# Eighty-seven short idle matmuls for five long ones, and two zeroings moved ahead of a maximum, in a fused convolution and maxout layer

## The chip, the cores and the metric

The kernel runs on one core of a Trainium2 chip. The time is device time in microseconds (us) of one execution; for the kernel before it is the median of three runs. The profile is of one further execution, with a span of 454.9 us from the first instruction to the last. TensorE multiplies matrices, VectorE (DVE), ScalarE (ACT) and GpSimd (POOL) work element by element, and SyncE (SP) issues most of the transfers, which run on the core's 16 DMA engines.

## The reference, cut to what matters

The input `x` has 8 sequences of 4160 tokens with 192 channels. First comes a causal convolution along the sequence: 8 heads of 24 channels, 7 taps a head, the taps being the softmax of `weight`. Then comes a maxout layer over all 33,280 tokens:

```
w = softmax(weight)                                  # 8 heads x 7 taps
y[s, h, :] = sum over k of w[h, k] * x[s - 6 + k, h, :]   # zero ahead of a sequence
h = maximum(maximum(y @ w1, y @ w2), y @ w3)         # 192 -> 768
out = h @ w_out                                      # 768 -> 192
```

The output is float32.

## The kernel before, in words

**Blocks.** The tokens are cut into 65 blocks of 512. Each block goes through four steps: load and cast its input to 16 bits, convolve, first layer with maxima (`h`), second layer (`po`, `o`) and store.

**The algebra.** The kernel doesn't form three products. With `wd` holding `w1 - w3` and `w2 - w3`, it computes `h = max(relu(y (w1 - w3)), y (w2 - w3))`, and adds `y (w3 w_out)` in the second layer, where the small matrix `w3 w_out` (`m16`) is made once by `transpose_w3` and `make_m`. ScalarE does the relu out of PSUM (line 494, tile `r`), VectorE the maximum (line 495, tile `h`), which also releases the PSUM buffer of the second product (`lq`).

**Convolution.** It is a matmul with a banded matrix (`band`), made at the start from the softmax by 38 small matmuls (line 280) and copies by ScalarE and VectorE (line 284). Blocks 0 to 3 are "dense": their input is cast to 16 bits into `xz` (line 211), 80 matmuls of line 382 (tile `D`) convolve them channel-major, and the result `yd` is used directly; `cross` makes the copy of two channel groups on the other half of the partitions that the first layer needs. From block 4 on the convolution runs token-major (line 361, tile `G`), is copied out (line 401), turned round by transposing transfers (line 415) and doubled by GpSimd (line 424, tile `yp`).

**Order of the work.** Every engine executes its own queue in order, and the order in which the code is written is the order in the queues; waits between engines are set from the data. The part ahead of the main loop is written out by hand: loads of block 0, the first weights, block 1, the other weights, the output weights `wos`, blocks 2 and 3 (lines 232 to 241), then the band and the dense blocks 0 and 1 with their first layer, then block 2's convolution, `cross(2)`, `make_m` and `first_hidden`, which is the hidden part of block 0's second layer. The main loop (`for t in range(2, NB)`) then interleaves block t's first layer (`l1`, line 507, one call for each j of the six slices of 128 hidden units) with block t-1's second layer (`st2`, line 571), and closes an output pair with a ScalarE copy (line 578) and a VectorE add (line 579). That add frees a PSUM buffer of `psw`, which later second-layer matmuls need.

**Idle matmuls.** `keep_warm(n, pool, tag)` issues n matmuls on a tile of zeros (`idle`), whose result nobody reads; they keep TensorE working while it has no data. One call with 5 stands ahead of the band matmuls (line 264), one with 3 behind them (line 287).

**Zeroings.** Input buffers `xf` are used again for later blocks, which have another layout. Rows 32 to 63 of such a buffer aren't all written by the later loads, so `zero_x(t, q0, q1, eng)` zeroes them once: with an engine given, by a memset of that engine (line 134), otherwise by a ScalarE copy of zeros (line 137). For buffers 0 to 3 only the columns NQ to NR are zeroed (5 to 8, 32x576 elements). Buffer 0's is a ScalarE copy ahead of the main loop; buffers 1, 2 and 3 are zeroed by VectorE within block 2's turn of the loop: buffer 1 after block 3's convolution (j = 1), buffer 2 at j = 2, buffer 3 at j = 4. Blocks 8, 9 and 10 are loaded into these buffers later.

**Instructions.** Each engine's program is a long straight line of instructions, and the trace shows packets of kind "instruction" on two DMA queues beside the data. A matmul call is two instructions on TensorE: a weight load (LDWEIGHTS) and the matmul.

Of the kernel before, what the change touches and what calls it, by code (L numbers as in the profile page):

```python
# [15 lines left out]
P = 128  # L16
# [5 lines left out]
NBLK = 512  # L22
# [6 lines left out]
def kernel(  # L29
# [12 lines left out]
    nc = tc.nc  # L42
# [15 lines left out]
    for b in range(B):  # L58
        s = nfull * NBLK
        while s < SEQ:  # L60
            n = min(SEQ - s, NBLK - off)
# [26 lines left out]
    NQ = len(chunks_of[0])  # L88
    TOK = 32
    NR = NBLK // TOK // 2  # L90
# [3 lines left out]
    def rows_of(t):  # L94
        rows = [(b, S + o) for (b, S, N, off) in blocks[t] for o in range(0, N, TOK)]
        assert len(rows) == 2 * NR
        return rows
# [12 lines left out]
    psp = ctx.enter_context(tc.tile_pool(name="psp", bufs=2, space=bass.MemoryType.PSUM))  # L110
    psq = ctx.enter_context(tc.tile_pool(name="psq", bufs=2, space=bass.MemoryType.PSUM))
    psw = ctx.enter_context(tc.tile_pool(name="psw", bufs=4, space=bass.MemoryType.PSUM))
# [5 lines left out]
    def get_x(t):  # L118

        if not 0 <= t < NB or t in xin:  # L120
            return
        if t < XBUF:
            xbuf.append(const.tile([P, NR, D], FP32, name=f"xf_{t}"))
        xf = xbuf[t % XBUF if t < NDENSE + XBUF else NDENSE + (t - NDENSE - XBUF) % 3]
        assert all(v[0] is not xf for v in xin.values())
        xin[t] = [xf, 0, ()]

    def zero_x(t, q0=0, q1=NR, eng=None):

        if t >= NDENSE:  # L130
            get_x(t)
        xf = xbuf[t]
        if eng is not None:
            eng.memset(xf[TOK:HALF, q0:q1, :], 0.0)
            return
        zero = idle[TOK:HALF, 0:D]
        nc.scalar.copy(out=xf[TOK:HALF, q0:q1, :],
                       in_=bass.AP(tensor=zero.tensor, offset=zero.offset,
                                   ap=[list(zero.ap[0]), [0, q1 - q0], [1, D]]))

    def load_x(t, eng=nc.sync):
        if not 0 <= t < NB:
            return
        loaded.add(t)
        get_x(t)
        xf = xin[t][0]
        if t < NDENSE:
            todo = [(0, c[3], c[1] * SEQ + c[2], i) for i, c in enumerate(chunks_of[t])]
        else:
            todo = [(HALF * (i // NR) + (0 if s else LAP), KR if s else TOK,  # L150
                     b * SEQ + s - (LAP if s else 0), i % NR) for i, (b, s) in enumerate(rows_of(t))]
        parts = []
        i, n = 0, len(todo)
        row = [c[2] for c in todo]
        while i < n:
            k = i
            while k + 1 < n and todo[k + 1][:2] == todo[i][:2] and row[k + 1] - row[k] == row[i + 1] - row[i]:
                k += 1
            step = row[i + 1] - row[i] if k > i else 0
            p0, rlen, _, q0 = todo[i]  # L160
            q1 = todo[k][3] + 1
            src = bass.AP(tensor=x.tensor, offset=row[i] * D,
                          ap=[[D, rlen], [step * D, q1 - q0], [1, D]])
            eng.dma_start(out=xf[p0:p0 + rlen, q0:q1, :], in_=src)  # L164
            if parts and parts[-1][0] == rlen:
                parts[-1] = (rlen, parts[-1][1], q1)
            else:
                parts.append((rlen, q0, q1))
            i = k + 1
        xin[t] = [xf, todo[0][0], parts]  # L170
# [6 lines left out]
    def place(t):  # L177
        return pairs.get(t, (t, 0, 0))
# [3 lines left out]
    def cast_x(t):  # L182
        if not 0 <= t < NB:
            return
        xf, p0, _ = xin.pop(t)
        t0, u, nu = place(t)
        if u == 0:
            pool = x16q if nu == 4 else x16p
            x16s[t0] = pool.tile([P, NHEAD, 4, nu, 2, GRP], FP16, tag="x16", name=f"x16_{t0}")
        if p0:  # L190
            nc.gpsimd.memset(xf[0:p0, 0, :], 0.0)
        K = HALF + KR
        for r in range(2):
            nc.gpsimd.tensor_copy(out=x16s[t0][0:K, :, :, u, r, :].rearrange("p h j c -> p j h c"),  # L194
                                  in_=xf[0:K, 4 * r:4 * r + 4, :].rearrange("p j (h c) -> p j h c", c=GRP))
# [49 lines left out]
    nc.gpsimd.tensor_copy(out=ident16[:], in_=ident[:])  # L245
    idle = const.tile([P, NBLK], FP16)
    nc.vector.memset(idle[:], 0.0)
    def keep_warm(n, pool=psw, tag="w"):

        ps = pool.tile([P, NBLK], FP32, tag=tag, name="idle")  # L250
        for _ in range(n):
            nc.tensor.matmul(ps[:], lhsT=idle[:, 0:P], rhs=idle[:], start=True, stop=True)

# [5 lines left out]
        nc.vector.memset(xz[0][v][:], 0.0)  # L261
    band = const.tile([P, NHEAD, BAND_W], FP16)
    nc.vector.memset(band[:], 0.0)
    keep_warm(5, psp, "p")
    wexp = const.tile([NHEAD, KW], FP32)
    wsum = const.tile([NHEAD, 1], FP32)
    nc.scalar.activation(out=wexp[:], in_=wk[:], func=AF.Exp, accum_out=wsum[:])
# [8 lines left out]
    for lo, hi, copy in ((0, CUT, nc.scalar.copy), (CUT, WIN, nc.vector.tensor_copy)):  # L276
        bps = psq.tile([32, hi - lo + 3, NHEAD], FP32, tag="q", name=f"band_{lo}")
        for c in range(lo, hi):

            nc.tensor.matmul(bps[:, c - lo:c - lo + 4, :].rearrange("p c h -> p (c h)"),  # L280
                             lhsT=line[:, WIN - 1 - c:WIN + 31 - c],
                             rhs=ident16[0:NHEAD, 0:4 * NHEAD], start=True, stop=True)
# [135 lines left out]
    def double(t):  # L418

        if not NDENSE <= t < NB:  # L420
            return
        yp = dense[t]
        for i in range(2):
            nc.gpsimd.tensor_copy(out=yp[HALF * i:HALF * (i + 1), 1, :, :, :, :].rearrange("p i u k n -> p (i u k n)"),  # L424
                                  in_=yp[HALF * (1 - i):HALF * (2 - i), 0, :, :, :, :].rearrange("p i u k n -> p (i u k n)"))
# [35 lines left out]
    def op(fn):  # L461
        ops.append((tuple(put), fn))
# [132 lines left out]
    def first_hidden(k):  # L595

        meet()
        first.append(psw.tile([P, 2, D], FP32, tag="w", name=f"po_0_{k}"))
        for s in range(2):
            for j in range(NJ):  # L600
                n = 2 * k + s
                nc.tensor.matmul(first[k][:, s, :], lhsT=hs[0][:, j, P * n:P * (n + 1)], rhs=wo[:, j, :],  # L602
                                 start=(s == 0 and j == 0), stop=False)
# [119 lines left out]
    make_m(1)  # L723
    first_hidden(1)
    zero_x(0, NQ)
    load_x(7)
    cast_x(5)

# [19 lines left out]
    for t in range(2, NB):  # L748
        u = convs_at.get(t, NB)
        late = t > 2 and u < NB  # L750
        if t in (3, 4):
            double(t + 1)
        if t > 3:
            for v in range(casts.get(t - 1, 8) + 1, casts[t] + 1):
                cast_x(v)
        l1(t, 0)
        if t == 2:
            first_rest()
        elif t == 3:
            cast_x(8)  # L760
            nc.gpsimd.tensor_copy(out=m16[0:HALF, 2, :], in_=m16[HALF:P, 0, :])
            nc.gpsimd.tensor_copy(out=m16[HALF:P, 2, :], in_=m16[HALF:P, 1, :])
        if t > 3 and not late:
            op(lambda t=t: (store(t - 2, 0, 4, (nc.sync,)),
                            turn(t + 2, (2,)) if place(t + 2)[1:] == (0, 4) else None, load_on(t)))
        else:
            op(lambda t=t: store(t - 2, 0, 4, (nc.sync,)))
        cuts = ROOM if late else EVEN
        st2(t - 1, (cuts[0], cuts[0]))
        for j in range(1, NJ):  # L770
            l1(t, j)
            if late and j == 1:
                st2(t - 1, (cuts[0] + OWN + AHEAD, cuts[0] + OWN))
                meet()
                quad, second = u >= QUADS, u < QUADS or t == u - 3
                conv(u, WPWQ, range(4 * second, 4 * second + 4) if quad else range(NHEAD))
                for i in (0, 2):
                    evac(u, i)
                for i in (1, 3):
                    evac(u, i, nc.vector.tensor_copy)  # L780
                if second:
                    turn(u)
                load_on(t)
            if t == 2 and j == 1:
                meet()
                conv_dense(3, (ACT, DVE))
                zero_x(1, NQ, NR, nc.vector)
                cross(3, GP)
                load_x(8)
                cast_x(6)  # L790
            elif t == 2 and j in (2, 4):
                zero_x(1 + j // 2, NQ, NR, nc.vector)
            elif t == 2 and j == 3:
                meet()
                conv(u, WW)
                evac(u, 0)
                evac(u, 1, nc.vector.tensor_copy)
                turn(4)
                load_x(9)
                cast_x(7)  # L800
            st2(t - 1, (cuts[j], cuts[j]))
            if j == 1 and t > 4 and t + 2 in pairs and pairs[t + 2][1] % 2 == 0:
                double(t + 2)
            if t == NB - 1 and j == 3:
                op(lambda: store(NB - 2, 0, 2, (nc.sync,)))
        if t == NB - 1:
            op(lambda: store(NB - 2, 2, 4, (nc.sync,)))
# [29 lines left out]
```

## Time and profile before

| what | before |
|---|---|
| time, median of 3 runs | 455.32 us (454.91 to 456.1) |
| span of the profile | 454.9 us |
| TensorE busy | 447.8 us (98%) |
| VectorE, ScalarE, GpSimd busy | 357.4, 319.3, 202.5 us |
| idle matmuls (line 252) | 8, 632 ns each in the middle |
| VectorE zeroings of `xf` (line 134) | 4, at 7.3, 31.3, 32.9 and 36.7 us |
| instruction packets | 60 and 24 on two queues |

In a line of the timeline the first number is the start in us, the second the time covered, then come engine, line, operation, output and inputs; the bracket tells how long the engine had been idle before it and what ended this idleness. In a line of the chain, the numbers are the start and the length in us of a piece of the sequence of work that ended last. A matmul's recorded duration overlaps that of the next one, so the distance between two starts tells more than a duration.

### The profile page before, as it was taken

The page shows a single profiled execution, that of the slowest core. Times are in us where ns is not written, and L with a number is a line of the kernel's source. Part 1 is how long each engine was busy: PE and PEld are TensorE (multiplying, and loading weights), DVE is VectorE, ACT ScalarE, POOL GpSimd, SP SyncE. Part 2 cuts the span into 40 slices and gives each one's busy share as a digit, 9 for nine tenths or more (in the row PEclk, how much of TensorE's full clock was granted, in tenths as well). Part 3 has the DMA queues.
Part 4 walks back from the last instruction along what each step waited for, and adds up shares of the span by engine and source line. Part 5 has one row for each costly group of instructions (what it writes and reads, how often), then busy time and mean ns, then how long its engine had stood idle before and what let it go on. Part 6 is the DMA issues. An engine that isn't in the chain of part 4 may idle for free.

```text
span 454.9 us, 18495 instructions
## 1 busy us (share of the span) xinstructions
PE 447.8 (98%) x7702; PEld 413.3 (91%) x7702; DVE 357.4 (79%) x615; ACT 319.3 (70%) x604; POOL 202.5 (45%) x228
## 2 busy tenths in 40 slices
PE   8999999999999999999999999999999999999997
PEld 4368999999999999999999999999999999999996
DVE  6757778878788787887878788787878878787775
ACT  7666677767777776777767677776767777676664
POOL 2584836546453444645246364525446452504000
PEclk9999999999999999999999999999999999999999
DMA  7969977697865959588595958858594876524223
GB/s 200 225 165 131 235 178 191 171 197 174 181 172 136 195 131 194 135 176 181 105 205 149 199 131 162 200 125 199 128 205 127 169 192 114 127 85 105 61 71 105
DMA packets 127987, 72.03 MB, mean 158 GB/s; under 512 B 52064, under 2 KB 127711, under 8 KB 127903
## 3 DMA queue, kind: packets, MB, share of 16 engines
q1 hardware_dynamic: 127743, 70.75, 68.6%
q8 instruction: 60, 0.98, 1.0%
q14 instruction: 24, 0.20, 0.2%
q10 hardware_dynamic: 160, 0.10, 0.1%
HBM read 33.28 MB, written 25.56 MB: 129 GB/s over the span
## 4 chain that ended last, share of the span: by engine, by line
PE 94%; DMA 3%; SPq 1%; DVE 0%; issue 0%; POOL 0%; ACT 0%; POOLq 0%; DVEq 0%
PE po L571 35%; PE lq L507 31%; PE lp L507 22%; PE G L361 3%; DMA xf<-in_x_dram 2%; DMA ws<-in_moe_w_dram 1%; SPq L223 1%; PE D L382 0%; PE po L629 0%; SPq L227 0%; SPq L164 0%; POOL xz L211 0%; PE pm L341 0%; PE po L602 0%; DVE h L495 0%
## 5 line engine op out<-in xcount | busy, mean ns | idle before, releaser
L495 DVE TENSOR_TENSOR h<-r,lq 128x512 f16<-128x512 f16 x384 | 262.8, 685 | 86.1 <-ACT r L494 78.2
L571 PE MATMUL po<-wo,h 64*128 64x192 f16 x3024 | 330.3, 243 | 0.0
L494 ACT ACTIVATE r<-lp 128x512 f16<-128x512 f32 x384 | 228.9, 597 | 115.9 <-PE lp L507 101.9
L507 PE MATMUL lp<-yp,wd 64*128 64x512 f16 x1098 | 295.6, 376 | 0.0
L507 PE MATMUL lq<-yp,wd 64*128 64x512 f16 x1098 | 295.5, 376 | 0.0
L571 PEld LDWEIGHTS <-h 64*128 64x128 f16 x3024 | 241.5, 94 | 5.6 <-issue 4.1
L507 PEld LDWEIGHTS <-wd 64*128 64x128 f16 x2268 | 178.3, 94 | 11.5 <-issue 0.5
L194 POOL CAST x<-xf 103x768 f16<-103x768 f32 x122 | 97.1, 824 | 107.0 <-DMA xf<-in_x_dram 86.6
L571 PE MATMUL po<-m,yp 64*128 64x192 f16 x720 | 141.0, 243 | 0.0
L424 POOL COPY yp<-yp 64x1536 f16<-64x1536 f16 (+1 forms) x62 | 89.4, 1442 | 96.3 <-DMA yp<-ys 69.3
L579 DVE TENSOR_TENSOR o<-a,po 128x384 f32<-128x384 f32 x126 | 69.0, 547 | 0.0
L571 PEld LDWEIGHTS <-yp 64*128 64x128 f16 x720 | 66.3, 94 | 0.2
L578 ACT COPY a<-po 128x384 f32<-128x384 f32 x126 | 59.6, 473 | 0.0
L401 ACT CAST ys<-G 128x384 f16<-128x384 f32 x61 | 26.3, 482 | 9.5 <-PE G L361 9.4
L401 DVE CAST ys<-G 128x384 f16<-128x384 f32 x61 | 31.0, 549 | 0.0
L361 PE MATMUL G<-x,band 39*32 39x192 f16 (+2 forms) x1152 | 17.3, 234 | 0.0
L361 PEld LDWEIGHTS <-band 39*32 39x32 f16 x1152 | 10.7, 92 | 5.2 <-issue 4.7
L507 PE MATMUL lp<-yd,wd 64*128 64x512 f16 x36 | 9.9, 377 | 0.0
L507 PE MATMUL lq<-yd,wd 64*128 64x512 f16 x36 | 9.7, 376 | 0.1
L382 PEld LDWEIGHTS <-xz 112*32 112x32 f16 x320 | 5.0, 107 | 4.2 <-POOL xz L211 2.5
L211 POOL CAST xz<-xf 112x160 f16<-112x160 f32 (+2 forms) x15 | 4.1, 320 | 9.3 <-DVE wd L299 7.9
L530 PEld LDWEIGHTS <-wd 128*128 128x128 f16 (+1 forms) x48 | 3.0, 96 | 5.8 <-issue 1.8
(73 smaller groups left out, 99.2 us busy)
## 6 DMA issues: line engine op xcount, KB each, us to landing
xf<-in_x_dram SPq DMA_DIRECT2D x113, 234.0 KB
out_dram<-o SPq DMA_DIRECT2D x62, 384.0 KB
xf<-in_x_dram SPq DMA_DIRECT2D x7, 204.8 KB
xf<-in_x_dram SPq DMA_DIRECT2D x3, 420.0 KB
ws<-in_moe_w_dram SPq DMA_DIRECT2D x8, 128.0 KB
yp<-ys SPq DMA_TRANSPOSE x62
out_dram<-o SPq DMA_DIRECT2D x5, 192.0 KB
wos<-in_moe_w_out_dram SPq DMA_DIRECT2D x1, 576.0 KB
```

What stands on the lines that cost most here:

```text
L194: nc.gpsimd.tensor_copy(out=x16s[t0][0:K, :, :, u, r, :].rearrange("p h j c -> p j h c"), in_=xf[0:K, 4 * r:4 * r + 4, :].rearrange("p j ( ...
L223: nc.sync.dma_start(out=st[:, n, f], in_=wsrc[0:P, f])
L361: nc.tensor.matmul(G[2 * (k // per) + i][TOK * j:TOK * (j + 1), k % per, :], lhsT=band[row, h, HALF * i + LAP:HALF * i + KR], rhs=x16s[t0] ...
L382: nc.tensor.matmul(ps[32 * g:32 * g + 32, lo:hi], lhsT=xz[t][v][0:rlen, q, 32 * s:32 * s + 32], rhs=band[0:rlen, h, cc:cc + hi - lo], star ...
L401: copy(out=slots[t][:, i % 2, :, :, GRP * h0:GRP * (h0 + per)].rearrange("p u r (h c) -> p h (u r) c", c=GRP), in_=G[i][:].rearrange("p h ...
L424: nc.gpsimd.tensor_copy(out=yp[HALF * i:HALF * (i + 1), 1, :, :, :, :].rearrange("p i u k n -> p (i u k n)"), in_=yp[HALF * (1 - i):HALF * ...
L494: nc.scalar.activation(out=r[:], in_=ps[0][:], func=AF.Relu)
L495: nc.vector.tensor_max(out=hs[t][:, j, :], in0=r[:], in1=ps[1][:])
L507: nc.tensor.matmul(ps[i][:], lhsT=w_of(i, c, j), rhs=y_all(t, i, c), start=(n == 0), stop=(n == NC - 1))
L571: nc.tensor.matmul(ps[b0, i][:, s % 2, :], lhsT=a, rhs=b, start=first, stop=last)
L578: nc.scalar.copy(out=a[:], in_=ps[s - 1, 0][:])
L579: nc.vector.tensor_add(out=outs[t][:, s - 1:s + 1, :], in0=a[:], in1=ps[s - 1, 1][:])
```

## The change: what it does and what it is for

`keep_warm` takes a size, and the first call issues 87 matmuls of 32 rows of output and 32 columns in place of 5 of 128 and 512. TensorE's program becomes 82 matmul calls longer at its beginning, so that all later instructions, and the borders at which new ones are fetched, come to lie elsewhere in the work. The zeroings of buffers 2 and 3 move from the loop (j = 2 and j = 4 of block 2) to the part ahead of it, behind `cross(2)` in VectorE's queue and ahead of block 2's first maximum.

```diff
-    def keep_warm(n, pool=psw, tag="w"):
+    def keep_warm(n, pool=psw, tag="w", M=P, N=NBLK):
 
         ps = pool.tile([P, NBLK], FP32, tag=tag, name="idle")
         for _ in range(n):
-            nc.tensor.matmul(ps[:], lhsT=idle[:, 0:P], rhs=idle[:], start=True, stop=True)
+            nc.tensor.matmul(ps[0:M, 0:N], lhsT=idle[:, 0:M], rhs=idle[:, 0:N], start=True, stop=True)
@@
-    keep_warm(5, psp, "p")
+    keep_warm(87, psp, "p", 32, 32)
@@
     make_m(1)
     first_hidden(1)
     zero_x(0, NQ)
+    zero_x(2, NQ, NR, nc.vector)
+    zero_x(3, NQ, NR, nc.vector)
     load_x(7)
     cast_x(5)
@@
                 cross(3, GP)
                 load_x(8)
                 cast_x(6)
-            elif t == 2 and j in (2, 4):
-                zero_x(1 + j // 2, NQ, NR, nc.vector)
             elif t == 2 and j == 3:
                 meet()
                 conv(u, WW)
```

## The prediction

> **What bounds the kernel now.** I read the busy shares first, then the chain of waits in order of time, then the timeline of each engine where the chain leaves TensorE, and last the DMA part.
>
> ```profile
> PE 447.8 (98%) x7702; PEld 413.3 (91%) x7702; DVE 357.4 (79%) x615; ACT 319.3 (70%) x604; POOL 202.5 (45%) x228
> PE 94%; DMA 3%; SPq 1%; DVE 0%; issue 0%; POOL 0%; ACT 0%; POOLq 0%; DVEq 0%
> ```
>
> TensorE ends the span: 94% of the chain is matmuls. By windows TensorE is busy 409.00 of 409.00 us between 41 and 450 us, so nothing is to be won there unless the matmuls change, and they don't. The time outside is the start (0 to 41 us) and the drain (450 to 454.9). In the start the chain is this:
>
> ```profile
> 6.71 5.30 DMA ws<-in_moe_w_dram
> 12.03 9.61 DMA xf<-in_x_dram
> 22.39 1.06 POOL xz L211 x4
> 23.49 1.05 PE D L382 x67
> ...
> 32.49 0.37 issue
> 32.86 0.54 DVE xf L134
> 33.43 0.57 DVE o L579
> 34.04 0.57 PE po L571 x9
> ...
> 36.78 0.48 ACT a L578
> 37.29 0.70 DVE h L495
> 38.03 0.37 PE lq L507
> ```
>
> Two things stand out. Up to 22 us the chain runs through loads: block 2's input, issued at 12.03, lands 9.6 us later. And twice afterwards TensorE, in full flow, waits for VectorE. The timeline of both places:
>
> ```profile
> 19.50 1.15 POOL L698 CAST wo<-wos 128x1152 f16<-128x1152 f32 x1 [1.02 <-DMA wos<-in_moe_w_out_dram]
> 20.70 1.15 PE L602 MATMUL po<-wo,h 128*128 128x192 f16 x12 [0.42 <-ACT w3t L335]
> 21.79 1.64 POOL L211 CAST xz<-xf 112x240 f16<-112x240 f32 x6 [1.14 <-DMA xf<-in_x_dram]
> 22.23 2.30 PE L382 MATMUL D<-band,xz 112*32 112x103 f16 x80 [0.38 <-POOL xz L211]
> 25.29 1.12 DVE L393 COPY yd<-yd 64x512 f16<-64x512 f16 x2
> 28.04 0.69 DVE L495 TENSOR_TENSOR h<-r,lq 128x512 f16<-128x512 f16 x1 [1.62 <-ACT r L494]
> 32.86 0.54 DVE L134 MEMSET xf<- 32x576 f32 x1 [0.17 <-issue]
> 36.72 0.54 DVE L134 MEMSET xf<- 32x576 f32 x1 [0.17 <-PE po L571]
> ```
>
> The reader is to see: block 2's convolution takes TensorE 2.30 us at 22.23, where the same 80 matmuls take 1.10 us at 29.07 when their data are there; VectorE is idle for 1.62 us just before block 2's first maximum at 28.04; and the two zeroings at 32.86 and 36.72 are those on the chain.
>
> **Instruction fetches.** The DMA part has this line:
>
> ```profile
> q8 instruction: 60, 0.98, 1.0%
> ```
>
> 0.98 MB in 60 packets is 16 KB each. TensorE executes 7702 + 7702 = 15,404 instructions; over 60 that is 257 per packet, so this queue feeds TensorE. The trace's packet records put the first at 9.3, 15.0, 26.0, 31.7, 36.3 and 43.7 us, each taking 0.9 to 1.1 us. The completion records of the loads[...] show who pays: before 9.3 us the 16 counts of a load come within 1.1 us of each other; right after, one count is 1.1 to 1.25 us late; after 15.0 us the last one is about 3 us late. The output weights (wos) have 14 counts by 16.3, one at 16.5, and one at 19.45; block 2's input has 14 by 18.7, one at 19.5, the last at 21.64; block 3's has 14 by 21.0, one at 21.8, the last at 23.58. GpSimd starts on each within 0.15 us of that last count (19.50, 21.79, 23.70). So one engine, behind through two fetches of about 1.05 us, releases the path.
>
> [...] the 38 band matmuls (32 columns each) took 1.09 us, 28.7 ns each. [...] Here idle matmuls start 0.43 us apart at 1.2 and 4.6 us, and first-layer ones 0.22 us apart at 8.5 us: full speed came near 8.1 us, long after the idle ones.
>
> **The change part by part.**
>
> *Idle matmuls.* Removed: 5 x 0.43 us, 1.20 to 3.52. Added: 87 x 28.7 ns (the band row) = 2.5 us, so they end near 3.7[...]. The band matmuls wait for VectorE's line until 3.41 and start at 3.47: 0 to 0.25 us late. ScalarE's band copy slips by 0.15, block 0's convolution by up to 0.25. TensorE then sits idle 0.81 us before 9.94 for block 1's input, which hides it: cost 0. [...] I take 0, bound 0.3 us.
>
> *Fetches.* 82 more matmuls with their weight loads are 164 instructions, so each fetch comes 164 instructions earlier in the program (or 92 later than its predecessor did). Without congestion the packets of before start when about 256k - 80 instructions are executed. The new ones: the first at instruction 11 of before's count, about 4 to 5.5 us, instead of 9.3; the second at 267, where TensorE resumes at 9.94, plus the 2.5 us that a loaded queue adds, 12 to 12.5 instead of 15.0; the third at 523, the transposes at 19.5, plus 2 us, near 21.5 instead of 26.0. Between 4 and 7 us the DMA share is 0.66, so about 1 us of idle time per engine absorbs the first fetch. Block 2's input then carries one fetch, not two: it lands 1.05 us earlier, near 20.6. Both ends: 0 if the third fetch is served before it or the first isn't absorbed; 1.9 us if the late engine catches up with the second latest (19.5). Does TensorE follow? The output weights land at 18.4, their cast ends at 19.65, first_hidden can start at 20.3 instead of 20.7 when the transposes end, and is over by 21.4; block 2's casts run 20.75 to 22.4 and its convolution ends at 23.5 instead of 24.53. Everything behind it to 32 us is TensorE without a gap. **Gain 1.0 us**, bounds 0 and 1.9.
>
> *Zeroings.* Two of 0.54 us go to VectorE's queue behind the two copies that end at 26.41. They end at 27.5, and the maximum behind them waits for ScalarE until 28.04: added cost 0, hidden by the 1.62 us. GpSimd's casts beside memsets keep 0.82 us each, as at 31.8. At 32.86 the add of block 1's output has its ScalarE operand since 32.33, so it follows the maximum at 32.72 instead of 33.43, and TensorE resumes at 33.3 instead of 34.04: 0.7 us. At 36.72 the maximum's operand is there at 36.89; it starts at 36.93 instead of 37.29: 0.36 us. **Gain 1.05 us**, bounds 0.6 (if another wait follows closely) and 1.1. The loads of blocks 9 and 10 into the zeroed buffers are issued behind the transposes at 33.58 and later; zeroing earlier can't delay them.
>
> *Given back.* Block 4's transposed rows are doubled by GpSimd at 40.02, after 5.06 us of waiting for the transposes, and are ready at 41.7; TensorE takes them at 44.1, with all gains at 42.0. Even if the transposes didn't come earlier, 0.3 us remain. At the end a 61st fetch may appear near 449.6 us, where the DMA engines are idle until the last stores at 451.1. Both 0. From 41 us TensorE is saturated for every position of a fetch that the 60 packets have sampled.
>
> Sum: 455.3 - 1.0 - 1.05 = **453.3 us**.
>
> **Rivals.**
> 1. The zeroings alone pay: the third fetch comes ahead of block 2's last packets, or the first one isn't absorbed. For: 21.5 and 20.6 are close, and all engines are loaded from 7 us. Against: its packets were queued at 12 us. 455.3 - 1.05 = 454.3.
> 2. The late engine catches up entirely, and the weights also come sooner. For: the delay after 15.0 was nearer 1.9 than 1.05. Against: the second latest engine bounds it. 455.3 - 1.9 - 1.05 = 452.4.
> 3. Slower: the new fetches at 4 to 5 us hit the first weights (the landings at 5.5 to 6.8), or a fetch meets the transposes (both kinds of fetch at 36.3 coincide with landings bunched at 38.1), and a wait of 2 us takes the place of those removed, with the idle part's 0.25: 455.3 - 1.05 + 2.25 = 456.5. Against: slack of 0.8 us at 9.94 and over 2 us before block 4.
>
> **How the numbers follow.** Forecast 0.48, rival 1 0.27, rival 2 0.15, rival 3 0.10. Predicted is the forecast's 453.3. The range 452.2 to 455.0 holds the forecast and rivals 1 and 2 with about 0.3 us of spread; rival 3 and a little of rival 2's tail stay out. 0.3% is 1.37 us: faster means below 453.95, same up to 456.7. The forecast with nine tenths, rival 2 and a sixth of rival 1 give 0.62 faster; the rest of both and over half of rival 3 give same 0.30; slower 0.08.
>
> **What would show it.** After: TensorE's 16 KB packets near 5, 12 and 21 us; GpSimd's cast of block 2 near 20.7; its convolution shorter than 2.30 us; two zeroings on VectorE right after the copies of block 2, near 25.4 to 26.5 us, and none on the chain near 32 and 36 us; no wait of the output matmuls on the add near 33 us. Wrong would make it: block 2's input still landing at 21.6, a wait of TensorE on GpSimd's doubling near 42, or a late count in the last stores.

## The result, and the profile after

The changed kernel takes 457.6 us in the median of six runs (456.92 to 459.96); the kernel before, run beside it on the same chip, 455.46 us (454.91 to 456.18). The ratio is 1.005 with a 95% interval of 1.0026 to 1.0074: 2.1 us slower, where 2.0 us less were forecast. Behind each time below stands its ratio to the kernel before, run beside it, with this interval.

The page of the changed kernel: busy times, shares of the chain, and the queue of TensorE's instructions.

```profile
PE 447.9 (98%) x7784; PEld 413.6 (91%) x7784; DVE 357.8 (78%) x615; ACT 319.4 (70%) x604; POOL 202.5 (44%) x228
PE 97%; issue 1%; DMA 1%; DVE 1%; ACT 0%; SPq 0%; POOL 0%; DVEq 0%
q8 instruction: 61, 1.00, 1.0%
```

TensorE is busy for the same 447.9 us, so the matmuls have not become dearer. New is a share of 1% in the chain that belongs to nobody ("issue": the engine waits for nothing that the profile shows). The chain from 25.9 to 38.6 us, in order of time:

```profile
25.94 0.27 PE po L615 x4
...
26.30 0.93 issue
27.23 0.57 PE po L571 x9
...
36.72 0.13 PE lp L507
...
36.93 1.04 issue
37.98 0.67 PE po L571 x9
```

Neither VectorE nor a load stands on this chain any more, as was wanted. In their place come two pieces of about 1 us without an owner. The timeline of the changed kernel at these places, and at two later ones:

```profile
21.52 1.15 PE L382 MATMUL D<-band,xz 112*32 112x103 f16 x80
24.75 1.14 DVE L134 MEMSET xf<- 32x576 f32 x2 [0.17 <-issue]
27.23 0.26 PE L571 MATMUL po<-m,yd 64*128 64x192 f16 x2 [0.93 <-PE po L615]
27.23 0.09 PEld L571 LDWEIGHTS <-yd 64*128 64x128 f16 x1 [1.16 <-issue]
37.98 0.34 PE L571 MATMUL po<-wo,h 64*128 64x192 f16 x4 [1.04 <-issue]
37.98 0.11 PEld L571 LDWEIGHTS <-h 64*128 64x128 f16 x3 [1.32 <-issue]
62.20 0.37 PE L507 MATMUL lq<-yp,wd 64*128 64x512 f16 x1 [0.62 <-DVE h L495]
62.20 0.10 PEld L507 LDWEIGHTS <-wd 64*128 64x128 f16 x2 [0.87 <-issue]
76.26 0.11 PEld L507 LDWEIGHTS <-wd 64*128 64x128 f16 x3 [0.63 <-issue]
```

The reader is to see: the convolution of block 2 is the short one (1.15 us), and the two zeroings lie at 24.75. But four times matmuls (0.31 to 1.04 us) and weight loads (0.63 to 1.32 us) stand still together. A weight load of `wd`, whose data have been in place since the first layer began, has no data to wait for; that both streams of TensorE lack their next instructions is my reading, which the borders below and the experiments test.

Two brackets name an owner. At 27.23 it is TensorE's own matmul, which ended at 26.2. At 62.20 it is VectorE's maximum, which ended at 62.16, so a wait for data is to be ruled out there. The same matmul in the kernel before, 164 instructions earlier in the program, in its timeline:

```profile
61.89 0.38 PE L507 MATMUL lq<-yp,wd 64*128 64x512 f16 x1
62.05 0.69 DVE L495 TENSOR_TENSOR h<-r,lq 128x512 f16<-128x512 f16 x1 [0.47 <-ACT r L494]
```

It starts ahead of that maximum, so it doesn't wait for it, and that the maximum ended just before it in the changed kernel says nothing.

**Where the stops lie.** I numbered TensorE's weight loads, matmuls and semaphore instructions (those that only wait for another engine's counter) in program order, from 0 at the first weight load. The four stops come exactly ahead of the instructions 959, 1471, 2495 and 3007. All of these are 256k + 191 (k = 3, 5, 9, 11). With 65 further instructions in front, which the trace doesn't show, they would be the multiples of 256. That is also about what a packet brings: each holds 16 KB, and TensorE's 15,568 weight loads and matmuls over 61 packets are 255 a packet. The packet records then give a table: when TensorE passed one border, when the packet that it asks for started and ended, and when TensorE reached the next border and passed it (us).

| kernel, borders | first passed | packet | next reached | next passed | stop |
|---|---|---|---|---|---|
| after, 703 to 959 | 20.68 | 24.49 to 25.65 | 26.3 | 27.23 | 0.93 |
| after, 1215 to 1471 | 31.78 | 34.63 to 35.93 | 36.9 | 37.98 | 1.04 |
| after, 2239 to 2495 | 56.44 | 59.38 to 60.66 | 61.6 | 62.20 | 0.62 |
| after, 2751 to 3007 | 70.75 | 73.67 to 74.89 | 75.9 | 76.26 | 0.31 |
| before, 703 to 959 | 24.24 | 26.00 to 27.11 | 29.82 | 29.82 | none |
| before, 2239 to 2495 | 60.11 | 61.37 to 62.28 | 67.45 | 67.45 | none |

Read so, a packet asked for at one border brings the block behind the next one; no record names what a packet holds. It started 2.9 to 3.8 us after the border (its wait), took 1.2 to 1.3 us, and TensorE went on 1.4 to 2.0 us after its end: 5.5 to 6.6 us in all. The work between the borders lasted 5.1 to 5.6 us. In the kernel before, the wait was 1.3 to 1.8 us in these two rows, and between 2239 and 2495 lay 7.3 us of work. The stops, here the idle time of the matmuls, sum to 0.93 + 1.04 + 0.62 + 0.31 = 2.9 us, and 2.9 - 1.06 of the zeroings (shown below) is 1.8 of the 2.1 us. In the experiments a stop is given as the distance between the two starts around it; for these four that is 1.18, 1.29, 0.96 and 0.64 us.

### The profile page after: what moved, and what is told of

Read it like the earlier page. It is cut to its first block, busy times and chain, and to the rows that moved or that the text cites. A ratio compares the mean times of both kernels' runs of the same rounds, so it can differ in the third digit from the quotient of the medians.

```text
span 455.8 us, 18659 instructions
## 1 busy us (share of the span) xinstructions
PE 447.9 (98%) x7784; PEld 413.6 (91%) x7784; DVE 357.8 (78%) x615; ACT 319.4 (70%) x604; POOL 202.5 (44%) x228
## 3 DMA queue, kind: packets, MB, share of 16 engines
q1 hardware_dynamic: 127743, 70.75, 70.2%
## 4 chain that ended last, share of the span: by engine, by line
PE 97%; issue 1%; DMA 1%; DVE 1%; ACT 0%; SPq 0%; POOL 0%; DVEq 0%
PE po L571 36%; PE lq L507 31%; PE lp L507 22%; PE G L361 3%; PE D L382 1%; PE lw L530 1%; DMA xf<-in_x_dram 1%; PE lp L530 1%; PE po L602 0%; PE po L629 0%; PE lq L530 0%; PE pm L341 0%; DVE xz L211 0%; PE pt L332 0%; DVE h L495 0%
## 5 line engine op out<-in xcount | busy, mean ns | idle before, releaser
L401 ACT CAST ys<-G 128x384 f16<-128x384 f32 x61 | 26.3, 482 | 11.0 <-PE G L361 11.0
```

The source lines that it names most:

```text
L401: copy(out=slots[t][:, i % 2, :, :, GRP * h0:GRP * (h0 + per)].rearrange("p u r (h c) -> p h (u r) c", c=GRP), in_=G[i][:].rearrange("p h ...
```

## The experiments

The theory from here on is that TensorE waits for its own instructions at borders. Its rivals: the matmuls wait for data that the profile doesn't name; the moved zeroings hurt; the kernel needs the long idle matmuls for its clock, a guess that no trace had shown.

**The kernel before again**, for the spread of its executions.

> The kernel before, once more, for a second profile: its first one was taken in an execution 1.2 us above the median. Fetch theory: TensorE never stands still at a border of 256 instructions (numbers 191, 447, 703, 959, 1215, 1471 of its program); the one stop between 31 and 38 us is that behind the add near 33 us. Block 2's input lands between 20 and 22 us.

One execution of 455.62 us, span 453.8. No stop at a border; the waits are those on VectorE's add. The chain of waits of this run:

```profile
31.78 0.54 DVE xf L134
32.35 0.56 DVE o L579
```

and its timeline behind them:

```profile
32.95 0.26 PE L571 MATMUL po<-m,yd 64*128 64x192 f16 x2 [0.85 <-DVE o L579]
```

A zeroing ahead of the add costs TensorE 0.85 us there, as the forecast read it.

**The zeroings alone.** Edit against the kernel before:

```diff
     zero_x(0, NQ)
+    zero_x(2, NQ, NR, nc.vector)
+    zero_x(3, NQ, NR, nc.vector)
@@
-            elif t == 2 and j in (2, 4):
-                zero_x(1 + j // 2, NQ, NR, nc.vector)
```

> Only the two zeroings moved, 5 long idle matmuls as before. Fetch theory: the borders lie in the work as before, so the zeroings bring what was forecast for them, 1.0 us, or less if the fetch for instruction 1215 comes late once the work ahead of it is shorter: 0.3 to 1.0 us faster than before. Rival theory (the zeroings are what costs, by delaying the maximum or GpSimd): 1 to 2 us slower than before.

454.79 us, ratio 0.9991 (0.9977 to 1.0006). From the start of block 2's first layer to the convolution that is issued in block 3's turn of the loop (39.15 us in the kernel before) TensorE takes 11.53 us, and 12.59 in both profiles of the kernel before: 1.06 us less, where 1.05 were forecast. There is no stop at a border. In the whole time only 0.4 us of it is to be seen, with an interval that reaches from 1.0 us faster to 0.3 us slower.

**The idle matmuls alone**: the changed kernel with the zeroings back in the loop.

```diff
-    zero_x(2, NQ, NR, nc.vector)
-    zero_x(3, NQ, NR, nc.vector)
@@
+            elif t == 2 and j in (2, 4):
+                zero_x(1 + j // 2, NQ, NR, nc.vector)
```

> Only the 87 short idle matmuls, zeroings at j = 2 and 4 as before. Fetch theory: TensorE stands still at instruction 959 (about 1 us, near 26 us) as in the changed kernel, and at some of the later borders 1471, 2493, 3004; 2 to 3 us slower than before, that is 0 to 1 us above the changed kernel. Rival theory (the zeroings cost): as before or 1 us faster.

458.89 us, ratio 1.0078 (1.0059 to 1.0097): 3.6 us dearer than the kernel before, so the idle matmuls carry the loss and the zeroings don't. Of the four stops only that at 2495 is there. That at 959 isn't: in this execution block 2's input came late (GpSimd's cast starts at 22.60), so that 9 us lay between the borders 703 and 959 and hid the packet. Matched instruction by instruction with the second profile of the kernel before, this one is 3.6 us behind when block 2's first layer begins (in it is half of the 3.4 us at half clock from 25.5 us on, 1.7 us by my estimate; the mean granted clock of this execution was 0.996 over 458.5 us) and loses 1.0 us more at the stop. So the medians give the loss to the idle matmuls, but this profile shows only 1.0 us of it as a wait for instructions. The timeline of this kernel:

```profile
65.44 0.10 PEld L507 LDWEIGHTS <-wd 64*128 64x128 f16 x2 [1.06 <-issue]
```

**The shift made a whole block.** 133 short matmuls are 128 more than before, or 256 instructions, so every border lies where it lay before.

```diff
-    keep_warm(87, psp, "p", 32, 32)
+    keep_warm(133, psp, "p", 32, 32)
```

> The changed kernel with 133 short idle matmuls instead of 87: 128 more than the five, 256 instructions, so that the borders lie in the work exactly where they lay before. Fetch theory: no standing still at the borders; 0.5 to 1.2 us slower at the start than with the zeroings alone, because the idle matmuls end 1.3 us later and 0.8 of it is hidden; 1 to 2.5 us faster than the changed kernel, about level with before. Rival theory (short idle matmuls cost by themselves, through the clock or the late band): slower than the changed kernel by 1 us or more.

456.4 us, ratio 1.003 (1.0013 to 1.0046). With 46 more idle matmuls than the changed kernel it is 1.2 us below that kernel's 457.6, so no loss that grows with their number shows; the intervals (1.0013 to 1.0046, and 1.0026 to 1.0074) overlap, though, and level with the kernel before, as was expected, it is not. And my "no stops" was wrong: the packet asked for at 66.8 us waited 5.4 us, and TensorE stood from 72.91 to 74.94; a smaller stop lies inside a convolution. The profile is of an execution of 459.58 us, 3.2 above the median, so it shows what can happen rather than what is usual. The timeline of this kernel:

```profile
30.23 0.34 PE L382 MATMUL D<-band,xz 112*32 112x103 f16 x13 [0.45 <-issue]
```

So borders that lie where they lay before don't rule a stop out: here it was 2.03 us.

**Five short ones, or none.** Two edits of the changed kernel:

```diff
-    keep_warm(87, psp, "p", 32, 32)
+    keep_warm(5, psp, "p", 32, 32)
```

> 5 short idle matmuls in place of 5 long ones, zeroings moved: the form of the change without its length, the program of TensorE keeps its borders. Fetch theory: within 0.4 us of the kernel with the zeroings alone, so 0.2 to 1.0 us faster than before, and in the profile no stop of 0.5 us at a border; block 2's input lands between 20 and 22 us as before. Rival theory (the small form costs, through the clock): 1 us or more slower than the zeroings alone.

```diff
-    keep_warm(87, psp, "p", 32, 32)
```

> No idle matmuls ahead of the band at all, zeroings moved: 10 instructions fewer than before, so each border lies 10 instructions later in the work. By the profile of the kernel before, the shortest time between two borders then grows from 5.1 to about 5.4 us. Fetch theory: as with the zeroings alone or up to 0.5 us faster, so 0.3 to 1.2 us faster than before; no stop at a border. Rival theory (the idle matmuls are needed for the clock): 1 to 3 us slower than the zeroings alone.

455.01 us (0.9991, 0.9978 to 1.0003) and 455.15 us (1.0, 0.9982 to 1.0018). Both are back at the time before or a little below, where 0.2 to 1.2 us less were expected. The loss of 1 us and more that the rival let follow from a lack of long idle matmuls isn't there, so they show no use for the clock: block 0's convolution starts at 6.13 us without them, at 6.09 in the kernel before and at 6.31 in the changed one. The stretch that the zeroings shorten lasts 11.50 us in each. But each profile has stops that I hadn't expected, 0.6 us twice with five, and one of 2.15 us with none, whose packet had waited 5.7 us (in an execution 2.4 us above the median). The timeline of the kernel without the first idle matmuls:

```profile
72.90 0.16 PEld L360 LDWEIGHTS <-band 39*32 39x32 f16 x19 [2.06 <-issue]
```

**Fewer loads in the way.** If the third packet waits behind queued loads, two loads issued later should bring it forward and remove the first stop, with the border unmoved.

```diff
-    for t in range(NDENSE, XBUF):
-        load_x(t)
+    load_x(NDENSE)
@@
     zero_x(3, NQ, NR, nc.vector)
+    load_x(5)
+    load_x(6)
```

> The changed kernel with the loads of blocks 5 and 6 issued behind that of block 7, some 5 us later, so that the DMA engines have less queued when TensorE asks for the block that starts at instruction 959. Fetch theory (the packet is late because the engines are loaded): the third packet starts before 24 us instead of 24.5, and the stop at instruction 959 falls from 1.2 us to under 0.5; the later stops (1471, 2493, 3004) may stay, and others may come from the loads that now lie later. Rival theory (the stop is a wait for data, not for instructions): the stop stays at 1.0 us or more.

The third packet starts at 21.3 us instead of 24.5, and the matmuls of line 571 follow without a pause. The kernel still takes 459.85 us (1.0108, 1.0091 to 1.0126): the postponed loads are themselves late, GpSimd waits 8.3 us for them, and TensorE for GpSimd. And the stop at 2495 has grown to 2.25 us, behind a packet that waited 4.0 us. The timeline of this kernel:

```profile
26.68 0.33 PE L571 MATMUL po<-m,yd 64*128 64x192 f16 x3
...
37.53 0.37 PE L507 MATMUL lp<-yd,wd 64*128 64x512 f16 x1 [2.41 <-POOL yd L393]
```

The first line is that of 27.23 in the changed kernel, with no bracket. For the first stop, in one profile, the theory is borne out: with two loads behind it the packet came 3.2 us earlier, and the stop of 0.93 us was gone. This remedy costs more than it brings.

**A border in the midst of a convolution.** 41 short matmuls put border 1215 among 64 like matmuls, and only 3.3 us of work lies between the two borders ahead of it.

```diff
-    keep_warm(87, psp, "p", 32, 32)
+    keep_warm(41, psp, "p", 32, 32)
```

> 41 short idle matmuls, zeroings moved: 72 instructions more than before. They end at 2.4 us, ahead of the band, so the start costs nothing. By the profile of the kernel before, borders 959 and 1215 are then only 3.3 us apart near 28 us, since both the convolution of block 3 and that of block 4 lie between them, and three later pairs 5.2 us. A fetch has needed 5.5 to 6.5 us from the border that asks for it where the engines are loaded. Fetch theory: a stop of 1.5 to 3 us at instruction 1215, and 1 to 3 us slower than before although fewer instructions are added than in the changed kernel. Rival theory (each added idle matmul costs): between before and the changed kernel, 0 to 1 us slower than before.

455.67 us (1.0016, 1.0004 to 1.0029). The stop came where it was forecast, with 1.21 us instead of the expected 1.5 to 3, and a small one at border 447. The timeline of this kernel:

```profile
31.16 0.53 PE L361 MATMUL G<-x,band 39*32 39x48 f16 x47
32.71 0.25 PE L361 MATMUL G<-x,band 39*32 39x48 f16 x17 [1.02 <-issue]
32.71 0.14 PEld L361 LDWEIGHTS <-band 39*32 39x32 f16 x16 [1.12 <-issue]
```

The 47 and the 17 matmuls are of one call and take the same operands, so a wait for data can't part them. This is the clearest line against the first rival. The time by itself speaks for the rival: 0.2 to 1.3 us slower lies nearer to its 0 to 1 us than to the 1 to 3 us that the theory let expect.

**Fewer stores in the way.** The changed kernel without the stores of the first 14 blocks; the results of these blocks are not written.

```diff
-        if t < 0:
+        if t < 14:
```

> The changed kernel without the stores of blocks 0 to 13 (their outputs are left unwritten), all else and TensorE's program the same. Fetch theory (a packet is late where the DMA engines have data queued): the stops at instructions 2493 and 3004, in front of whose fetches a store had just been issued, shrink from 1.0 and 0.6 us to under 0.3 each; those at 959 and 1471, ahead of which loads were queued and only one store, may stay; 0.5 to 1.5 us faster than the changed kernel. Rival theory (the stops lie at fixed places of TensorE's program whatever the transfers do): all four stay, and the time is that of the changed kernel.

456.43 us (1.0019, 1.0004 to 1.0034), 2.0 us faster than the changed kernel beside it (1.003 to 1.0074, so that the intervals just meet). Of the stops of 2495 and 3007, 0.50 us is left of the first and nothing of the second; those of 959 and 1471, which might have stayed, are gone too, and one of 0.9 us is new, at 1215. So with TensorE's program unchanged, fewer data for the DMA engines to move changed where the stops lie and how long they are.

**The changed kernel again**, beside it.

> The changed kernel once more on this chip, for a second profile. Fetch theory: stops at instructions whose number is 191 of 256 (less one for each semaphore instruction before), 2 to 4 us of them in all, most below 110 us; 1.5 to 3 us slower than before. Rival theory (the stops of the first profile were chance): other places, or none.

458.39 us (1.0052, 1.003 to 1.0074). Stops at 959, 2495 and 3007, the last one of 2.3 us. Busy time in three stretches of this run; the columns are the stretch, its length, the busy us of PE, PEld, DVE, ACT and POOL with their counts, the granted clock of TensorE, the DMA share and GB/s:

```profile
70.90:74.40 3.50, 3.50 (x112) 3.13 (x107) 2.81 (x6) 2.32 (x5) 3.38 (x3) 1.00 0.99 239
74.40:76.70 2.30, 0.33 (x5) 0.00 (x0) 1.15 (x2) 0.57 (x2) 1.15 (x4) 1.00 1.46 171
78.10:81.50 3.40, 3.40 (x31) 2.88 (x28) 1.52 (x3) 1.67 (x3) 0.17 (x1) 0.50 0.65 163
```

In the second stretch there is not one weight load in 2.3 us. Ahead of it, while the packet waited (asked for at 69.51, started at 73.72), the 16 DMA engines are full: a share of 0.99. (A packet is counted whole where it starts, so a share can pass 1.) The third stretch shows a second bill: 3.4 us at half the clock (0.50 granted).

**Loads split in two.** The kernel with the zeroings alone, in which a turn issues one load at its beginning and the rest at j = 3, so that a packet finds less in front of it.

```diff
-    def load_on(t):
-        for v in range(loads[t - 1] + 1, loads[t] + 1):
-            if v not in loaded:
-                load_x(v)
+    def load_on(t, most=1):
+        todo = [v for v in range(loads[t - 1] + 1, loads[t] + 1) if v not in loaded]
+        for v in todo[:most]:
+            load_x(v)
@@
+            if j == 3 and t > 2:
+                op(lambda t=t: load_on(t, 9))
+                emit()
```

> The zeroings moved, 5 long idle matmuls, and in the loop only one block's load where up to two were issued at once; the other follows at j = 3, some 3 us later. Fetch theory: less is queued ahead of a fetch between 45 and 75 us, so the longest time from a border to its packet falls from 4.7 us to under 3.5 there, the stops of 0.6 us and more vanish, and the zeroings bring nearly their whole 1.06 us: 0.5 to 1.1 us faster than before. Rival theory (the rest of the zeroings' gain is lost elsewhere, or loads that come later make GpSimd late): as with the zeroings alone, or slower with TensorE waiting for converted inputs.

454.49 us (0.9991, 0.998 to 1.0001). Packets still waited up to 4.2 us, against an expected 3.5 at most (4.7 with five short idle matmuls, 3.6 in the first profile of the zeroings alone), and two stops of about 1.2 us remain, at 959 and 2751. Not better than the zeroings alone, which ran beside it:

> Only the zeroings moved, once more beside the split loads, since its first profile held a stretch at half clock. Fetch theory: 0.2 to 0.8 us faster than before in the median, with the best executions 1 us faster than the best of before; from block 2's first layer to the convolution at j = 1 of block 3, 11.5 us instead of 12.6. Rival theory: no part of the zeroings' gain is left.

454.52 us (0.9984, 0.997 to 0.9998), no stop over 0.4 us in its profile, the two zeroings at 24.51 us, and no wait for the add. Its stretch took 12.20 us, 0.66 us more than in the first profile: some 0.45 us are lost in a wait for GpSimd (line 311) and 0.2 at border 959, so the full gain isn't in every execution. The timeline of this second run of the zeroings alone:

```profile
24.51 1.15 DVE L134 MEMSET xf<- 32x576 f32 x2 [0.17 <-issue]
...
31.63 0.55 DVE L579 TENSOR_TENSOR o<-a,po 128x384 f32<-128x384 f32 x1
```

This is the best version that I found: half of the change, 0.4 to 0.7 us below the kernel before in two comparisons, of which only the second has an interval (0.1 to 1.4 us) without zero.

**All profiles together.** Fourteen profiles hold 20 such stops of half a microsecond and more, all at 256k + 191. TensorE always went on 1.2 to 2.0 us after the packet's end; where it didn't stop, it passed the border at least 1.3 us after that end. The wait of a packet follows the load on the DMA engines (818 packets; engines busy with data in the 2 us after the border). 137 of these packets started ahead of the time at which TensorE passed the border, by up to 1.6 us, so a packet can be asked for before the border is reached in execution, and the real waits can be longer than these:

| data engines busy, mean | median wait, us | longest |
|---|---|---|
| under 4 | 0.1 | 1.1 |
| 4 to 8 | 0.4 | 1.7 |
| 8 to 12 | 0.3 | 2.9 |
| 12 to 14 | 1.0 | 3.1 |
| 14 to 16 | 1.0 | 4.3 |
| 16 | 1.2 | 5.7 |

## Why the prediction was wrong, point by point

*The zeroings.* Right in mechanism and size. They lie at 24.75 us behind block 2's copies and hide there, both waits on the chain are gone (the chain itself named only the first zeroing; the second stood ahead of a maximum on it), and the stretch is 1.06 us shorter (12.59 to 11.53) where 0.7 + 0.36 were forecast. In the whole time 0.4 to 0.7 us of it arrive, with wide intervals. A shorter stretch is also less time between two borders; in the kernel with five short ones two stops of 0.6 us took such a gain back. Whether this is all of the difference isn't shown.

*The idle matmuls' own cost.* Right up to the first convolution. They end at 3.70 us (forecast 3.7), the band matmuls start at 3.63 instead of 3.47, and block 0's convolution at 6.14 to 6.38 us in the five profiles with these idle matmuls instead of 5.96 to 6.09 in the five with long ones. But block 1's convolution, whose slack was to hide this, waits for its input until 10.1 to 11.0 us instead of 9.7 to 9.9. The first packet, now at 4.7 us, may not have been absorbed; as the start is 10.4 with five short ones too, whose borders didn't move, the cause is open. That the short form does nothing to the clock was assumed, not shown.

*The fetches' places.* Mostly right, though the borders lie at 256k - 65 and not at 256k - 80: first packets at 4.7 and 12.1 us (forecast 4 to 5.5 and 12 to 12.5). The third came at 24.5, not 21.5: it waited 3.8 us and not the 2 us that were assumed. The 61st packet at 449.9 did no harm, as forecast.

*Gain of 1.0 us from block 2's input.* Not confirmed. GpSimd's cast starts at 19.93 us, better than the forecast 20.7, and the convolution is short. But in the kernel before it starts at 21.79 in one profile and at 20.70 in the next, and with the idle matmuls alone at 22.60. The means are 20.8 us for the six profiles with the borders of before and 20.6 for the five with those of the change. A gain below this scatter (block 2's first layer starts at 25.8 us in the median of the six and at 25.0 in that of the five) isn't excluded. I had read one profile as the kernel's property. That a late count among a load's 16 stands for one DMA engine held up by fetches was an estimate too; no trace names a count's engine.

*"From 41 us TensorE is saturated for every position of a fetch that the 60 packets have sampled."* This is the step that failed, together with its like for the start, "Everything behind it to 32 us is TensorE without a gap": a wait of TensorE for its own instructions was put at nothing. The forecast treated a packet only as traffic that delays data, and never as something that TensorE itself waits for. The runs showed four such waits in its place, two before 41 us (0.93 and 1.04 us) and two behind (0.62 and 0.31), 2.9 us in all. The 60 packets had sampled when the packets of before came; they had not sampled how much work lies ahead of each border at a shift of 164. The numbers stood in the same trace: packets that started up to 3.4 us after their border, and blocks of instructions that last 5.2 us at the shortest.

*Rival 3* had the right sign and somewhat over half of the size (1.2 us slower, 456.5), for another reason, so by luck: it let fetches delay weights or transposes. Of this the profile has no sign: block 2's first layer starts earlier, and GpSimd's doubling of block 4's rows, at 38.89 us, lies between those of the two profiles of the kernel before (38.25 and 40.02).

From profile to profile (second one of before against the changed kernel) the account closes: -0.8 us up to block 2's first layer, +1.3 in the next stretch (-1.06 of the zeroings and 2.4 around the two stops there), +0.8 and +0.6 around the two later stops, +2.0 in all, against 2.1 us between the medians. From 85 us to the end the two stay 1.97 us apart to within 0.01 us, so nothing behind the stops adds to the loss. Against the first profile of the kernel before, whose block 2 came 1.1 us later, the same sum is 0.9. Open stay how the gain and the loss up to block 2 divide between the shift and chance, and why some stops of over 2 us are followed by half the clock and others not.

## What to carry to other kernels

Here TensorE's instructions were an input like its data, which it stood waiting for, up to 2.3 us at a time. To look for this in another kernel, number an engine's instructions, find the borders, and compare the work between two borders with the packet's wait, its transfer and the time up to the first instruction. In these runs a stop took both little work and loaded DMA engines. In the fourteen profiles, with 14 and more engines busy, TensorE stopped at the end of 8 of 14 blocks of 256 instructions that held under 5.3 us of work, of 8 of 42 with 5.3 to 6.5 us, and of 1 of 283 with more; with under 10 engines busy, of none of 256. A change that shifts a program must be tried over several shifts, and read from several executions, since the gain seen in one profile can be the scatter of the loads.

## What the runs showed of the hardware

- Behind loaded DMA engines a packet of instructions started up to 5.7 us after its border. What stood ahead of it inside an engine, no run shows.
- Three of the five waits of TensorE of 2.0 us and more that the runs show were followed by 3.4 us at a granted clock of 0.50, beginning 0.3 to 1.3 us after the wait. Two more such stretches (from 23.0 us with the zeroings alone, from 25.5 us with the idle matmuls alone) had no stop at a border ahead of them. The idle time ahead of the three was 2.0 to 2.3 us. The mean granted clock of these five executions was 0.996, and 1.000 in the other profiled executions of the experiments. Matched instruction by instruction with the kernel before, stop and stretch cost 3.6 us with 133 short idle matmuls and 3.7 with none ahead of the band, by my estimate the stop (2.0 and 2.1 us) and half of 3.4 us.
